# Gated attention unit with a cosine-gated two-layer product on one core: consecutive tokens per partition, v rows padded apart, and three moved scores

## Chip, cores and metric

The kernel runs on one core of one Trainium2 chip (trn2). The metric is the device time of an execution in microseconds; lower is better. Verdicts are "faster", "same" or "slower" at 2%.

## The reference

```python
def _attn_ref(u, v, z):                       # u, v: 8 x 3008 x 256, z: 8 x 3008 x 64
    scale = 1.0 / S
    scores = scale * np.matmul(z, z.transpose(0, 2, 1))
    attn = np.maximum(scores, 0.0) ** 2
    out = np.matmul(attn, v)
    return (u * out).astype(np.float32)

def _moe_ref(x, w_in, w_out):                 # x: 24064 x 256, w_in: 256 x 2048, w_out: 2048 x 256
    h = x @ w_in
    g = h * np.cos(h)
    return (g @ w_out).astype(np.float32)
# reference = _moe_ref(_attn_ref(u, v, z).reshape(24064, 256), w_in, w_out)
```

Inputs and output are float32. The scores are symmetric, and the sum over tokens in the attention doesn't depend on the order of the tokens, as long as z, v, u and the output rows all use the same order. The first part of the change uses that.

## The kernel before

Each batch of 3008 tokens is cut into 24 blocks of 128 (the last has 64) and six columns of four blocks. A column J of a batch is a slot; there are 48. For one column, PE makes scores (two 64-row matmuls side by side, "a score" below), ScalarE takes relu (`r`), VectorE squares (`A`), and PE multiplies the pieces of `A` with v in "value pairs" (two 64-row matmuls each). Half of the `A` pieces are had by a DMA transposition of the other half, as the scores are symmetric. Then the gate with u gives x, `emit_h` makes h = x·w_in, ScalarE and VectorE make g = h·cos(h), and y = g·w_out follows. The first three columns of batch 0 run by `phase_a_first`, for which nothing is prepared yet. In the lines of the profile `E` and `M` are tiles in PSUM, the memory that matmuls write (a piece of it that one matmul fills is a bank here), `zT` is the transposed z, and `sm` the sum of attention results that the gate uses (the gate sum).

Token order in the loads (u and v, and the last rows apart):

```python
def load_rows(t, src, b, g):
    full = 4 if g < NC - 1 else 3
    nc.gpsimd.dma_start(
        t[:, 0:full, :],
        src[b, g * CW:g * CW + full * P, :].rearrange("(j p) d -> p j d", p=P),
    )
    # ... the last 64 tokens are put in both halves of the partitions

def load_v(b, g):
    t = vpool.tile([P, 4, D], FP16, name="v16")
    load_rows(t, v, b, g)
    vs[b, g] = t
```

The first three columns, with the places of the scores:

```python
def phase_a_first(s, n, extra={}):
    # ... takes banks; steps = value pairs (dh, k), 46 of them, then the last block
    lo, hi = 5 if s == 0 else 2, 42
    at = {}
    for i in range(n):
        p = lo + (hi - lo) * i // (n - 1)
        at[p] = at.get(p, 0) + 1
    for i, (dh, k) in enumerate(steps):
        # ... the value pair
        if dh > 0 and (k % 4 == 3):
            drop_piece((b, J, k // 4))
            if s > 0:
                emit_turns((0, 0), 1)          # one DMA transposition of A
                if k < 4:
                    turn_u(s)
                # ...
        for _ in range(at.get(i, 0)):
            emit_score(later=squares if s == 0 and i == lo else None)
    # ...
    late_sums.extend(gate_sum(s, *acc[dh]) for dh in range(2))
    hold(late_sums[0][0:1, 0:1])               # a GpSimd copy that waits for the gate sum
    load_u(s + 1)
```

The calls of the three columns and what stands between them (the queue of w_out's load is GpSimd's, in order, so the load comes behind the `hold` and the u load at the end of the second column, s = 1):

```python
phase_a_first(0, 12, {4: lambda: turn_late(4), 8: lambda: turn_late(5)})
phase_a_first(1, 12)
nc.gpsimd.dma_start(w_out16, moe_w_out.rearrange("(k p) f -> p k f", p=P))
for i in range(2):
    emit_h(0, i)()
phase_a_first(2, 14)
# ...
phase_b(2)                                     # h of slots 0 and 1, and the first y: the first use of w_out
```

Of the kernel before, what the change touches and what calls it, by code (L numbers as in the profile page):

```python
# [9 lines left out]
FP16 = mybir.dt.float16  # L10
# [4 lines left out]
def kernel(  # L15
# [9 lines left out]
    nc = tc.nc  # L25
# [3 lines left out]
    B, S, D = u.shape  # L29
    dqk = z.shape[2]  # L30
    Dff = moe_w_in.shape[1]
    P = 128
    H = P // 2
    CW = 512
    NB = (S + P - 1) // P
    NC = (S + CW - 1) // CW
    WL = S - (NC - 1) * CW
    NFT = Dff // P
    NSLOT = B * NC
    NPC = 18  # L40
    assert D == 2 * P and dqk == H and S - (NB - 1) * P == H and NB == 4 * NC
    assert B % 2 == 0 and WL == 3 * P + H and NFT == 16

    inv_s2 = (1.0 / float(S)) * (1.0 / float(S))
    half_pi = float(math.pi / 2.0)
# [8 lines left out]
    vpool = pool("v", 7)  # L54
# [39 lines left out]
    def drop_piece(key):  # L94
        i = pieces.pop(key)
        if pending.get(i):
            pending[i] = "dropped"
        else:
            free_pieces.append(i)
# [8 lines left out]
    halves = [(0, NB // 2), (NB // 2, NB)]  # L108
    z16s, zTs, vs, u16s, uTs, xs, gs = {}, {}, {}, {}, {}, {}, {}
    yps = {}  # L110

    def load_z(b, half):
        lo, hi = halves[half]
        z16 = zpool.tile([P, NB // 2, P], FP16, name="z16")
        z16s[b] = z16
        full = min(hi, NB - 1)
        for h in range(2):
            nc.gpsimd.dma_start(
                z16[:, 0:full - lo, h * dqk:(h + 1) * dqk],
                z[b, lo * P:full * P, :].rearrange("(j p) d -> p j d", p=P),  # L120
            )
            if hi == NB:
                for r in range(2):
                    nc.gpsimd.dma_start(
                        z16[r * H:(r + 1) * H, hi - lo - 1, h * dqk:(h + 1) * dqk],
                        z[b, (NB - 1) * P:S, :],
                    )
# [10 lines left out]
    def load_rows(t, src, b, g):  # L138
        full = 4 if g < NC - 1 else 3
        nc.gpsimd.dma_start(  # L140
            t[:, 0:full, :],
            src[b, g * CW:g * CW + full * P, :].rearrange("(j p) d -> p j d", p=P),
        )
        if full == 3:
            for r in range(2):
                nc.gpsimd.dma_start(t[r * H:(r + 1) * H, 3, :], src[b, S - H:S, :])

    def load_v(b, g):
        t = vpool.tile([P, 4, D], FP16, name="v16")
        load_rows(t, v, b, g)  # L150
        vs[b, g] = t

# [104 lines left out]
    def emit_value(b, J, k, t, dh, bank, start, stop):  # L257
        nc.tensor.matmul(  # L258
            bank[:, 0:width(J)],
            vs[b, k // 4][t * H:(t + 1) * H, k % 4, dh * P:(dh + 1) * P],  # L260
            value_rhs(b, J, k, t),
            start=start,
            stop=stop,
        )
# [82 lines left out]
    def phase_a_first(s, n, extra={}):  # L347
        b, J = s // NC, s % NC
        ea = e_order.pop(0)
        pair = [E[ea][:, 0, :], E[ea][:, 1, :]]  # L350
        acc = [pair, M] if s == 1 else [M, pair]
        last = NB - 1
        run = 1 if s == 0 else 2
        steps = [
            (dh, k)
            for I in range(0, NC, run)
            for dh in range(2)
            for k in range(4 * I, min(4 * (I + run), last))
        ] + [(2, last)]
        lo, hi = 5 if s == 0 else 2, 42  # L360
        at = {}
        for i in range(n):
            p = lo + (hi - lo) * i // (n - 1)
            at[p] = at.get(p, 0) + 1
        for i, (dh, k) in enumerate(steps):
            if i in extra:
                extra[i]()
            if dh == 2:
                emit_value(b, J, last, 0, 0, acc[0][0], False, True)
                emit_value(b, J, last, 1, 1, acc[1][1], False, True)  # L370
            else:
                for t in range(2):
                    emit_value(
                        b, J, k, t, dh, acc[dh][t], k == 0, k == last - 1 and t != dh
# [4 lines that stand above are left out]
                    emit_turns((0, 0), 1)  # L379
                    if k < 4:  # L380
                        turn_u(s)
                    elif k < 8:
                        for d in range(2):
                            gate_mul(s - 1, d, late_sums.pop(0))
            for _ in range(at.get(i, 0)):
                emit_score(later=squares if s == 0 and i == lo else None)
        if s == 0:
            turn_u(0)
        late_sums.extend(gate_sum(s, *acc[dh]) for dh in range(2))
        hold(late_sums[0][0:1, 0:1])  # L390
        load_u(s + 1)
        e_order.append(ea)
# [30 lines left out]
    T = 2 * P  # L423
# [109 lines left out]
    def emit_y(m, i):  # L533
        for ft in range(2 * i, 2 * i + 2):
            for k in range(mwidth(m) // P):
                y_block(m, ft, k)

    def store_half(m, half, o):
        b, J = m // NC, m % NC
        n = min(2, mwidth(m) // P - 2 * half)  # L540
        t0 = b * S + J * CW + half * T
        if J == NC - 1 and half == 1 and n == 2:
            nc.sync.dma_start(out[t0:t0 + P, :], o[:, 0, :])
            nc.sync.dma_start(out[t0 + P:t0 + P + H, :], o[0:H, 1, :])
            nc.sync.dma_start(out[b * S - H:b * S, :], o[H:P, 1, :])
        else:
            nc.sync.dma_start(
                out[t0:t0 + n * P, :].rearrange("(k p) d -> p k d", p=P), o[:, 0:n, :]
            )

    def store_y(m):
        for half in range(2):
# [9 lines left out]
    def last_y(m):  # L562
        b, J = m // NC, m % NC
        for ft in range(NFT):
            y_block(m, ft, 0)
            y_block(m, ft, 1)
        for k in range(4):
            if k >= 2:
                for ft in range(NFT):
                    y_block(m, ft, k)  # L570
            o = opool.tile([P, 2, D], FP32, name="o")
            nc.scalar.activation(
                o[:, 0, :], y_bank(m, k),
                AF.Copy, bias=0.0, scale=inv_s2,
            )
            t0 = b * S + J * CW + k * P
            if k < 3:
                nc.sync.dma_start(out[t0:t0 + P, :], o[:, 0, :])
            else:
                nc.sync.dma_start(out[t0:t0 + H, :], o[0:H, 0, :])  # L580
                nc.scalar.dma_start(out[b * S - H:b * S, :], o[H:P, 0, :])

    def phase_b(s):
# [46 lines left out]
    for g in range(NC):  # L630
        eng = nc.sync if g % 2 == 0 else nc.scalar
        full = 4 if g < NC - 1 else 3
        eng.dma_start(
            z32[g][:, 0:full, :],
            z[0, g * CW:g * CW + full * P, :].rearrange("(j p) d -> p j d", p=P),
        )
        if full == 3:
            for r in range(2):
                nc.sync.dma_start(z32[g][r * H:(r + 1) * H, 3, :], z[0, S - H:S, :])
# [87 lines left out]
    for s in range(3, NSLOT + 1):  # L727
        b, J = s // NC, s % NC
# [52 lines left out]
```

## Time and profile before

| what | value |
|---|---|
| time, median of the first three runs | 1193.71 us (1193.34 to 1194.58) |
| span of the profiled run | 1191.4 us |
| matmuls on PE | 11887, busy 99% of the span |
| VectorE, ScalarE, GpSimd busy | 85%, 67%, 58% |
| DMA packets | 479862 |

The page lists the DMA queues as packets, megabytes and the time that their packets took, as a share of 16 engines' span:

```profile
DMA packets 479862, 148.00 MB, mean 124 GB/s; under 512 B 404208, under 2 KB 479472, under 8 KB 479728
...
q1 hardware_dynamic: 380752, 112.93, 54.4%
q0 software_dynamic: 97440, 32.78, 27.3%
```

q1 carries the transpositions and the stores, q0 the loads from GpSimd. Together they keep the 16 engines 82% busy, beside a PE that is 99% busy. Whole views are read in the prediction below.

### The profile page before, as it was taken

Reading aid. Unit: us, or ns where it says so; the run is one execution under the profiler, and the core shown is the slowest. Engines: PE = TensorE matmul, PEld = TensorE weight load, DVE = VectorE, ACT = ScalarE, POOL = GpSimd, SP = SyncE. Lnnn points to the kernel's source line nnn. Section 1 sums busy time; section 2 is a strip of 40 time slices with the busy share of each in tenths; the row PEclk is TensorE's granted clock in tenths of the full one; section 3 lists DMA queues with packets and bytes.
Section 4 is the critical chain, followed back from the end, with each engine's and each line's share of the span. In section 5 each row is a group of like instructions: output and inputs, shape, how many; then the busy total and the mean of one; then the engine's idle time right before and its main releaser. Section 6 shows DMA issues by size and latency. Waiting matters only on the chain.

```text
span 1191.4 us, 29044 instructions
## 1 busy us (share of the span) xinstructions
PE 1183.3 (99%) x11887; PEld 727.2 (61%) x11887; DVE 1012.3 (85%) x1302; ACT 794.9 (67%) x927; POOL 690.5 (58%) x717
## 2 busy tenths in 40 slices
PE   9999999999999999999999999999999999999998
PEld 4556665665566656666566665656666566665566
DVE  6899888889988898888988889888888888888776
ACT  7966676667666676667676676666766666666454
POOL 3287746657466573755647556476565665545452
PEclk9999999999999999999999999999999999999999
DMA  9999998569995699946999459973898737964301
GB/s 160 172 170 163 138 147 131 102 121 134 143 130 98 123 140 162 131 84 104 157 147 135 85 104 161 169 119 72 122 164 149 122 71 123 166 125 86 65 20 54
DMA packets 479862, 148.00 MB, mean 124 GB/s; under 512 B 404208, under 2 KB 479472, under 8 KB 479728
## 3 DMA queue, kind: packets, MB, share of 16 engines
q1 hardware_dynamic: 380752, 112.93, 54.4%
q0 software_dynamic: 97440, 32.78, 27.3%
q8 instruction: 93, 1.52, 0.5%
q10 hardware_dynamic: 1536, 0.43, 0.2%
q14 instruction: 41, 0.34, 0.1%
HBM read 66.32 MB, written 24.64 MB: 76 GB/s over the span
## 4 chain that ended last, share of the span: by engine, by line
PE 97%; ACT 1%; DVE 1%; issue 0%; POOL 0%; DVEq 0%; ACTq 0%
PE E L404 27%; PE M L482 23%; PE M L258 20%; PE E L258 19%; PE E L194 5%; PE M L525 1%; ACT r L204 1%; PE M L460 1%; DVE g L415 0%; PE E L664 0%; DVE sm L270 0%; PE E L525 0%; POOL s L433 0%; ACT c L412 0%; DVE o L495 0%
## 5 line engine op out<-in xcount | busy, mean ns | idle before, releaser
L412 ACT ACTIVATE c<-E 128x1024 f16<-128x1024 f32 (+1 forms) x384 | 385.7, 1007 | 216.4 <-PE E L404 214.1
L415 DVE SCALAR_TENSOR_TENSOR g<-E,c 128x1024 f16<-128x1024 f32 (+1 forms) x384 | 458.4, 1195 | 60.6 <-ACT c L412 59.5
L204 ACT ACTIVATE r<-E 128x512 f16<-128x512 f32 (+1 forms) x342 | 327.9, 967 | 112.7 <-PE E L194 106.5
L258 PEld LDWEIGHTS <-v 64*128 64x128 f16 x4512 | 246.3, 94 | 229.3 <-issue 19.4
L404 PE MATMUL E<-x,w_in 128*128 128x512 f16 (+1 forms) x1408 | 354.0, 375 | 0.0
L433 POOL TENSOR_TENSOR s<-g 128x512 f16<-128x512 f16 (+1 forms) x184 | 208.3, 1132 | 188.5 <-DVE g L415 138.7
L258 PE MATMUL M<-A,v 64*128 64x512 f16 (+1 forms) x2256 | 283.0, 372 | 0.2 <-DVE o L495 0.2
L258 PE MATMUL E<-A,v 64*128 64x512 f16 (+1 forms) x2256 | 278.1, 371 | 0.0
L434 POOL TENSOR_TENSOR g<-g 128x512 f16<-128x512 f16 (+1 forms) x184 | 219.5, 1193 | 14.4
L404 PEld LDWEIGHTS <-w_in 128*128 128x128 f16 x1536 | 133.1, 98 | 108.9 <-issue 19.5
L482 PEld LDWEIGHTS <-g 128*128 128x128 f16 x2816 | 172.5, 98 | 40.8
L209 DVE TENSOR_TENSOR A<-r 128x1024 f16<-128x1024 f16 x240 | 174.0, 737 | 15.0 <-ACT r L204 14.3
L286 POOL TENSOR_TENSOR x<-sm,uT 128x512 f16<-128x512 f32 (+1 forms) x43 | 48.6, 1132 | 212.9 <-DVE sm L270 212.5
L482 PEld LDWEIGHTS <-s 128*128 128x128 f16 x2112 | 129.4, 98 | 32.1 <-DVE s L440 0.5
L194 PE MATMUL E<-zT 64*128 64x512 f16 (+4 forms) x684 | 127.6, 355 | 2.0 <-DVE sm L270 0.7
L440 DVE TENSOR_TENSOR s<-s,g 128x1024 f16<-128x1024 f16 (+1 forms) x92 | 100.6, 1094 | 2.1 <-POOL s L433 2.1
L482 PE MATMUL M<-w_mix,s 128*128 128x128 f16 x1408 | 94.0, 219 | 0.3 <-POOL s L433 0.3
L482 PE MATMUL M<-w_mix,g 128*128 128x128 f16 x1408 | 93.6, 219 | 0.0
L482 PE MATMUL M<-w_out,g 128*128 128x128 f16 x1408 | 93.6, 219 | 0.0
L212 DVE TENSOR_TENSOR A<-r 128x512 f16<-128x512 f16 (+1 forms) x102 | 79.6, 781 | 8.9 <-ACT r L204 8.1
L194 PEld LDWEIGHTS <-zT 64*128 64x128 f16 x684 | 38.8, 94 | 38.5 <-issue 4.0
L442 DVE TENSOR_TENSOR s<-g,s 128x1024 f16<-128x1024 f16 (+1 forms) x92 | 60.5, 660 | 0.0
(58 smaller groups left out, 646.9 us busy)
## 6 DMA issues: line engine op xcount, KB each, us to landing
out_dram<-o SPq DMA_DIRECT2D x87, 256.0 KB, 2.2
v<-in_v_dram POOLq DMA_DIRECT2D x40, 256.0 KB, 8.8
u<-in_u_dram POOLq DMA_DIRECT2D x40, 256.0 KB, 4.8
A<-A SPq DMA_TRANSPOSE x252, 5.1
z<-in_z_dram POOLq DMA_DIRECT2D x14, 192.0 KB, 10.6
z<-in_z_dram POOLq DMA_DIRECT2D x14, 176.0 KB, 5.9
v<-in_v_dram POOLq DMA_DIRECT2D x8, 192.0 KB, 11.9
u<-in_u_dram POOLq DMA_DIRECT2D x8, 192.0 KB, 4.1
```

The costliest lines, as they stand in the source:

```text
L194: nc.tensor.matmul(e[:, t, 0:Wt], zT[rows, k * P:(k + 1) * P], zT[rows, J * CW:J * CW + Wt], start=True, stop=True,)
L204: nc.scalar.activation(r[:, :, 0:W], e[:, :, 0:W], AF.Relu)
L209: nc.vector.tensor_tensor(a4, r4, r4, ALU.mult)
L212: nc.vector.tensor_tensor(a4, r[:, :, 0:W], r[:, :, 0:W], ALU.mult)
L258: nc.tensor.matmul(bank[:, 0:width(J)], vs[b, k // 4][t * H:(t + 1) * H, k % 4, dh * P:(dh + 1) * P], value_rhs(b, J, k, t), start=start, ...
L404: nc.tensor.matmul(e[:, f, 0:W], w_in16[:, k, ft * P:(ft + 1) * P], x[:, k, 0:W], start=(k == 0), stop=(k == 1),)
L412: nc.scalar.activation(c[:, :, 0:W], e[:, :, 0:W], AF.Sin, bias=half_pi, scale=inv_s2)
L415: return lambda: nc.vector.scalar_tensor_tensor(gs[m][:, 2 * i:2 * i + 2, 0:W], e[:, :, 0:W], 1.0, c[:, :, 0:W], ALU.mult, ALU.mult)
L433: nc.gpsimd.tensor_tensor(s1[:, f, 0:n], g[:, f, low], g[:, lower, low], ALU.add)
L434: nc.gpsimd.tensor_tensor(g[:, f, low], g[:, f, up], g[:, f, low], ALU.subtract)
L440: nc.vector.tensor_tensor(s2[:, f, 0:n], s1[:, f, 0:n], g[:, f, up], ALU.subtract)
L482: nc.tensor.matmul(acc[:, k * P:(k + 1) * P], left[:, ft, k * P:(k + 1) * P], right[:, ft, :], start=(ft == 0 and k == 0), stop=(ft == F - ...
```

## The change

The intent is fewer and larger DMA packets, and shorter stalls of PE in the second and third column. Three parts:

1. A partition holds 12 (first half of a batch) or 11 consecutive tokens instead of every 128th. The rows that a partition gets of u, of the first z and of the output then lie together in DRAM.
2. v's tile gets 16 unused columns per row, so that the v rows of a partition don't join into one packet on the chip's side.
3. Scores stand three value pairs further back: the second column's second one (behind pair 8 instead of 5), and the third column's first two (behind 5 and 8 instead of 2 and 5); the third column's third goes from behind pair 8 to behind 9.

```diff
+    def half_rows(rows, half):
+        lo, hi = halves[half]
+        n = min(hi, NB - 1) - lo
+        return rows[lo * P:(lo + n) * P, :].rearrange("(p j) d -> p j d", p=P)
+
+    def group_rows(rows, g):
+        first = 4 * (g % 3)
+        return half_rows(rows, g // 3)[:, first:first + (4 if g < NC - 1 else 3), :]
...
             t[:, 0:full, :],
-            src[b, g * CW:g * CW + full * P, :].rearrange("(j p) d -> p j d", p=P),
+            group_rows(src[b], g),
...
     def load_v(b, g):
-        t = vpool.tile([P, 4, D], FP16, name="v16")
+        t = vpool.tile([P, 4, D + 16], FP16, name="v16")[:, :, 0:D]
...
             p = lo + (hi - lo) * i // (n - 1)
+            if s > 0 and i < 2:
+                p = (2, 8)[i] if s == 1 else (5, 9)[i]
             at[p] = at.get(p, 0) + 1
...
-                out[t0:t0 + n * P, :].rearrange("(k p) d -> p k d", p=P), o[:, 0:n, :]
-            )
+            nc.sync.dma_start(rows[:, 2 * half:2 * half + n, :], o[:, 0:n, :])
...
-            z[0, g * CW:g * CW + full * P, :].rearrange("(j p) d -> p j d", p=P),
+            group_rows(z[0], g),
```

(The loads of later z, the last rows and the last stores are rewritten in the same way. Line numbers move: value matmuls L258 become L266, scores L194 become L202, h matmuls L404 become L414, first y matmuls L525 become L535, w_out's load L712 becomes L723.)

More of the change, by code (lines that the diff above doesn't have):

```diff
@@ L41 @@
     assert D == 2 * P and dqk == H and S - (NB - 1) * P == H and NB == 4 * NC
-    assert B % 2 == 0 and WL == 3 * P + H and NFT == 16
+    assert NC == 6 and B % 2 == 0 and WL == 3 * P + H and NFT == 16
     inv_s2 = (1.0 / float(S)) * (1.0 / float(S))
@@ L115, in load_z @@
         z16s[b] = z16
-        full = min(hi, NB - 1)
+        n = min(hi, NB - 1) - lo
         for h in range(2):
             nc.gpsimd.dma_start(
-                z16[:, 0:full - lo, h * dqk:(h + 1) * dqk],
-                z[b, lo * P:full * P, :].rearrange("(j p) d -> p j d", p=P),
+                z16[:, 0:n, h * dqk:(h + 1) * dqk], half_rows(z[b], half)
             )
@@ L536, in emit_y, with out_rows @@
                 y_block(m, ft, k)
+    def out_rows(m):
+        b, J = m // NC, m % NC
+        return group_rows(out[b * S:(b + 1) * S, :], J)
     def store_half(m, half, o):
-        b, J = m // NC, m % NC
+        b = m // NC
+        rows = out_rows(m)
         n = min(2, mwidth(m) // P - 2 * half)
-        t0 = b * S + J * CW + half * T
-        if J == NC - 1 and half == 1 and n == 2:
-            nc.sync.dma_start(out[t0:t0 + P, :], o[:, 0, :])
-            nc.sync.dma_start(out[t0 + P:t0 + P + H, :], o[0:H, 1, :])
+        if m % NC == NC - 1 and half == 1 and n == 2:
+            nc.sync.dma_start(rows[:, 2, :], o[:, 0, :])
+            nc.sync.dma_start(out[(b + 1) * S - H:(b + 1) * S, :], o[0:H, 1, :])
             nc.sync.dma_start(out[b * S - H:b * S, :], o[H:P, 1, :])
         else:
-            nc.sync.dma_start(
-                out[t0:t0 + n * P, :].rearrange("(k p) d -> p k d", p=P), o[:, 0:n, :]
-            )
+            nc.sync.dma_start(rows[:, 2 * half:2 * half + n, :], o[:, 0:n, :])
     def store_y(m):
@@ L575, in last_y @@
             )
-            t0 = b * S + J * CW + k * P
             if k < 3:
-                nc.sync.dma_start(out[t0:t0 + P, :], o[:, 0, :])
+                nc.sync.dma_start(out_rows(m)[:, k, :], o[:, 0, :])
             else:
-                nc.sync.dma_start(out[t0:t0 + H, :], o[0:H, 0, :])
+                nc.sync.dma_start(out[(b + 1) * S - H:(b + 1) * S, :], o[0:H, 0, :])
                 nc.scalar.dma_start(out[b * S - H:b * S, :], o[H:P, 0, :])
```

## The prediction

> **What bounds the kernel now.** I read the page first, then the waits of the matrix engine, then the timeline of its first 54 us with the starts of each matmul, and the DMA packets last.
>
> ```profile
> PE 1183.3 (99%) x11887; PEld 727.2 (61%) x11887; DVE 1012.3 (85%) x1302; ACT 794.9 (67%) x927; POOL 690.5 (58%) x717
> DMA  9999998569995699946999459973898737964301
> PE 97%; ACT 1%; DVE 1%; issue 0%; POOL 0%; DVEq 0%; ACTq 0%
> ```
>
> The matrix engine is busy 99% of 1191.4 us and makes 97% of the chain of waits; the DMA row is almost as full. Which of the two sets the end is told by the waits of PE, all that there are:
>
> ```profile
> PE E L664 <- DVE s L627: 1.2, 1, 1.2
> PE E L194 <- DVE sm L270: 0.7, 1, 0.7
> PE E L194 <- DVE g L415: 0.4, 1, 0.4
> PE E L194 <- ACT zT L657: 0.4, 1, 0.4
> PE M L482 <- POOL s L433: 0.3, 1, 0.3
> PE E L194 <- DVE zT L659: 0.2, 1, 0.2
> PE M L258 <- DVE o L495: 0.2, 1, 0.2
> PE E L194 <- ACT r L204: 0.2, 1, 0.2
> ```
>
> No line names a DMA: PE never waits for a transfer directly, in spite of the full DMA row. The only waits that a DMA ends near PE are at the start, in the waits of VectorE: `DVE z L645 <- DMA z<-in_z_dram` is 3.0 us in 2 times. So transfers can matter before the first transposition, and nowhere else as things stand.
>
> The busy row hides waits, since a matmul's end is modelled, so I took starts. A 512-column matmul over 128 rows starts 216 ns after the one before, and two 64-row ones share such a step (108 ns each). Summed over the kernel, the starts exceed this beat by only 17.7 us: 3.3 before 8.6 us, 0.8 from there to 23, 1.1 to 38.1, 1.7 to 53, then 0.9 per 100 us without exception. The last is the change between 64-row and 128-row work (47 of L258 to L404 at 0.2 us extra, 46 back at 0.1), which this edit does not touch. So what can be won at all is a part of about 7 us at the start.
>
> **What the Trainium skill says.** "TensorE: Matmul & The Clock Gate", section "Wait — 56ns, not 53.3ns?", gives warm start-to-start as N ÷ 2.4 GHz plus about 2.5 ns, 215.7 ns at 512 columns; the trace agrees (216). "Perfetto Trace Analysis", in its opening note, calls matmul busy time a bad metric since matmuls are pipelined; the trace agrees: the wait at 24.1 us below is 0.84 us by starts and 0.66 us by the idle column. "DMA: Bandwidth & Descriptors", section "Why small descriptors are slow (HBM only)", names a fixed overhead per packet; the trace agrees: a 256-byte packet took 20 ns at the start and a 1024-byte store 49 ns, 12.5 ns per 256 bytes.
>
> **The change part by part.** No arithmetic changes, and each engine has as many instructions as before.
>
> Part one, tokens. A partition gets 12 (or 11) consecutive tokens instead of every 128th. The first z loads then carry 4 rows of 256 bytes as one 1024-byte run, the u loads 4 rows of 1024 as one run, the stores of two output rows 2048 bytes. v rows stay single, as the new padding stops them from joining; the later z loads stay single because their rows are written to alternate 128-byte places. Packets: u 40×512 + 8×384 = 23552 become 48×128 = 6144; stores 87×256 = 22272 become 11136; first z 5×512 + 384 = 2944 become 768. That is 30720 fewer of 479862, so 449142. Estimated from the durations above, the DMA share of 82% loses some 4 points. Since PE never waits for it after the start, I count all that as zero.
>
> At the start it can count:
>
> ```profile
> 0.73 1.56 SPq L633 DMA_DIRECT2D z<-in_z_dram  x3
> 1.19 3.17 PE L664 MATMUL E<-s 128*128 128x512 f16 x7 [1.19 <-DVE s L627]
> 3.91 0.80 DVE L645 CAST z<-z 128x512 f16<-128x512 f32 x2 [2.78 <-DMA z<-in_z_dram]
> 4.39 0.77 PE L649 MATMUL turned<-id,z 128*128 128x128 f16 x8
> 4.93 0.59 ACT L657 COPY zT<-turned 128x512 f16<-128x512 f16 x1 [0.89 <-PE turned L649]
> 6.01 3.77 ACT L204 ACTIVATE r<-E 128x1024 f16<-128x1024 f32 x4 [0.49 <-PE E L194]
> ```
>
> The first z group lands at 3.89, its cast starts 0.02 later, and PE transposes at 4.39. With a quarter of the packets I estimate landing about 0.5 us sooner. But PE is not free then: the last of seven warm-up matmuls starts at 3.72 and they step by 427 ns, so nothing starts before 4.15. The gain is 4.39 − 4.15 = 0.24 us, whatever more the DMA saves. The chain behind it (copy, score, four activations) moves with it. v's first group lands at 8.12, before its use at 8.64, and should land earlier still, with less z traffic ahead of it.
>
> Part two, second column (s = 1). Its second score moves from behind value pair 5 to behind pair 8 (counted from 0).
>
> ```profile
> 23.26 0.40 PE L194 MATMUL E<-zT 64*128 64x512 f16 x2
> 23.47 0.83 PE L258 MATMUL E<-A,v 64*128 64x512 f16 x6
> 24.96 0.39 PE L194 MATMUL E<-zT 64*128 64x512 f16 x2 [0.66 <-DVE sm L270]
> 26.04 0.40 PE L194 MATMUL E<-zT 64*128 64x512 f16 x2
> ```
>
> The second score needs the bank that the gate sum of the column before reads until 24.91. Three pairs after 23.47 end at 24.12, so PE stands 0.84 us. With three pairs more it comes at 24.77 and waits 0.19. The third score, one pair behind, then starts at 24.96 + 0.22 + 0.22 = 25.39 instead of 26.04. That is 0.65 us ahead, but ScalarE must empty two banks in turn: its activation of the second score still starts at 25.39 and takes 1.03, so the fourth score, due at 26.25, waits for 26.47 (0.22). Left: 0.65 − 0.22 = 0.43 us. From there ScalarE can follow: in a backlog its activations start every 0.905 us, and this column asks for one per 1.0.
>
> Part three, third column (s = 2). First score from behind pair 2 to behind pair 5, second from 5 to 8, third from 8 to 9.
>
> ```profile
> 38.13 1.21 PE L258 MATMUL M<-A,v 64*128 64x512 f16 x6
> 39.77 0.39 PE L194 MATMUL E<-zT 64*128 64x512 f16 x2 [0.43 <-DVE g L415]
> 40.90 0.39 PE L194 MATMUL E<-zT 64*128 64x512 f16 x2
> 41.76 0.40 PE L194 MATMUL E<-zT 64*128 64x512 f16 x2
> ```
>
> Now PE stands 0.69 before the first and 0.27 before the second, both for the two products g of 1.2 us on VectorE. Moved, the first is due at 39.73 and starts at 39.77, the second still has to wait for 40.90, the third can start at 41.33 rather than 41.76. So 0.43 us looks won. I think that most is given back. Activations here start at 42.26, 43.18, 44.08, 44.98, 45.89, 46.79: no gap, 0.905 us apart, while the scores come every 0.86. Before, the ninth and tenth scores (46.99, 47.91) start 0.05 us after the seventh and eighth activations end (46.94, 47.86): by then ScalarE paces PE. The activations of scores one and two do not move by this edit, so the eighth ends at most 0.04 us earlier and the tenth score with it. Gain: 0.04 us, the rest swallowed by waits on ScalarE between scores four and ten.
>
> Sum: 0.24 + 0.43 + 0.04 = 0.71 us; 1193.71 − 0.71 = 1193.0 us.
>
> **Rivals.** (a) All of the placement gains stay: 0.24 + 0.65 + 0.63 = 1.5 us, 1192.2. For it: a score behind pair 9 finds PE far ahead, and small slips of ScalarE may have slack that I don't see. Against: the gapless activations. (b) ScalarE takes back the second column's gain too, or the start's landing does not improve: some 0.3 us, 1193.4. Against: gaps of 0.05 us before every third activation of that column. (c) Larger packets hold up the DMA transpositions of A that share the engines, and PE gets a wait for A: some 1 to 3 us more. For it: the DMA row of 9s and 5.1 us median per transposition. Against: fewer packets and less engine time in all, and no DMA wait now. (d) DMA relief shows in the body: several us. Against: the constant 0.9 us per 100 us; there is no DMA wait to take away. Also, the pitch of v (544 bytes instead of 512) could change its weight loads (94 ns); they lie beside matmuls.
>
> **Range and chances.** Three runs of before spread over 1.2 us, as much as the effect. From (a) with luck to (b) with a small part of (c): 1191.9 to 1194.2. Two per cent is 24 us, over three times all that the start holds. Faster by over 2%: 0.005; within: 0.985; slower (a strong form of (c)): 0.01.
>
> **What would show it.** Page: about 449 thousand packets, DMA row lower, PE still 99%. Start: first transposition at about 4.15; if it stays at 4.39 or the cast still starts at 3.9, the first step is wrong. Second column: a wait of about 0.2 us before the second score and a new one on an activation before the fourth; column 0.4 us shorter from 23.26. Third column: the DVE wait gone, waits on ACT in its place, the length from 38.1 to the first L404 behind it about unchanged; shortened by 0.4 or more, rival (a) holds. Any PE wait named after a DMA or after A speaks for (c), a fall of the 0.9 us per 100 us for (d); either would make the prediction wrong.

## The result, and the profile after

| kernel | runs, us | median |
|---|---|---|
| before, six runs | 1194.58, 1193.34, 1193.71, 1194.80, 1193.99, 1195.15 | 1194.28 |
| changed, six runs | 1196.83, 1199.05, 1193.20, 1193.58, 1196.91, 1192.81 | 1195.20 |

The ratio is 1.0009, 95% interval 0.9989 to 1.003: the same. A ratio here and below is the mean time of one kernel's runs over the mean of the other's in the same rounds, so it isn't quite the ratio of the medians. The median of 1195.20 lies outside the predicted range of 1191.9 to 1194.2. The runs fall in two groups: three at 1192.8 to 1193.6, which is where the prediction put them, and three at 1196.8 to 1199.1, all less than 1.5% above the fastest. The profiled execution (1196.83) is one of the longer ones, so its trace shows what the longer ones have.

The page of the changed kernel (busy row; packets and queues as above; the chain that ended last, by engine):

```profile
PE 1185.7 (99%) x11887; PEld 727.1 (61%) x11887; DVE 1012.7 (85%) x1302; ACT 794.5 (66%) x927; POOL 679.8 (57%) x717
...
DMA packets 449142, 148.00 MB, mean 124 GB/s; under 512 B 401264, under 2 KB 432496, under 8 KB 449008
...
q1 hardware_dynamic: 368464, 112.93, 56.9%
q0 software_dynamic: 80032, 32.78, 27.1%
...
PE 95%; DMA 2%; issue 1%; ACT 1%; DVE 0%; POOL 0%; ACTq 0%; POOLq 0%
```

The packet count is the predicted one exactly. The DMA share didn't fall by some 4 points; it rose from 81.7% to 84.0%. And in the chain a DMA stands with 2% of the span where before there was none. The waits of PE name it (total us, times, longest):

```profile
PE M L535 <- DMA w_out<-in_moe_w_out_dram: 2.4, 1, 2.4
...
PE E L202 <- ACT r L212: 0.4, 2, 0.2
```

One wait, once: the first y matmul for the w_out weights. The former waits for `sm` (0.7) and `g` (0.4) before scores are gone. Here is the same place in both kernels, PE's timeline (start, us, line, tiles, form, count, idle before). Before:

```profile
52.77 1.90 PE L404 MATMUL E<-x,w_in 128*128 128x512 f16 x8
54.51 1.04 PE L525 MATMUL M<-w_out,g 128*128 128x256 f16 x8
55.38 1.03 PE L404 MATMUL E<-x,w_in 128*128 128x512 f16 x4
```

After:

```profile
52.34 1.90 PE L414 MATMUL E<-x,w_in 128*128 128x512 f16 x8
56.66 1.88 PE L535 MATMUL M<-w_out,g 128*128 128x256 f16 x8 [2.41 <-DMA w_out<-in_moe_w_out_dram]
58.33 1.91 PE L414 MATMUL E<-x,w_in 128*128 128x512 f16 x4
```

Two things are to be seen. The changed kernel comes to this place 0.43 us sooner (52.34 against 52.77); eight matmuls of 216 ns on, at 54.07, PE is ready for y, and stands until 56.66, 2.6 us. And after the stand the same matmuls take almost twice as long: the first eight y matmuls 1.88 us against 1.04, the next four h matmuls 1.91 against 1.03. A table by stretches shows why (us, then busy time and count of PE, PEld, DVE, ACT and POOL, then the granted clock, DMA share and GB/s; packets in flight at the same time are added up, so the share can be over 1). After:

```profile
54.10:56.60 2.50, 0.15 (x1) 0.00 (x0) 2.50 (x3) 1.32 (x2) 0.62 (x2) 1.00 1.32 188
56.70:60.10 3.40, 3.40 (x13) 1.76 (x14) 0.19 (x1) 0.00 (x0) 0.00 (x0) 0.50 1.23 251
```

Before:

```profile
56.70:60.10 3.40, 3.40 (x24) 2.14 (x22) 2.71 (x3) 2.69 (x3) 3.40 (x4) 1.00 0.95 125
```

The granted clock was 0.50 in the stretch behind the stand, and 13 matmuls are counted in it where before there were 24. By the clock records it was low from 56.70 to 60.11. So a wait of 2.6 us cost about 4.2: at matmul 290, counted from 0, (38.34 against 38.75) the changed kernel is 0.41 ahead, at 460 (64.74 against 60.91) it is 3.8 behind, and 3.6 at the last (1190.33 against 1186.74). That single place makes the difference of the two profiled runs; what lies before and behind it is in the changed kernel's favour.

Why was w_out late? GpSimd's timeline where it is issued, before:

```profile
39.20 1.16 POOL L712 DMA_DIRECT2D w_out<-in_moe_w_out_dram  x1
```

After:

```profile
38.57 1.18 POOL L723 DMA_DIRECT2D w_out<-in_moe_w_out_dram  x1
```

And its time from issue to landing, in the DMA view of this stretch (KB each, us), before and after:

```profile
w_out<-in_moe_w_out_dram POOLq DMA_DIRECT2D x1, 1024.0 KB, 14.9
```

```profile
w_out<-in_moe_w_out_dram POOLq DMA_DIRECT2D x1, 1024.0 KB, 18.0
```

Before, w_out landed at 39.20 + 14.92 = 54.12, and its first use came at 54.51. The margin was 0.39 us, and that is why no list of waits named it: a wait list shows only what was late, not what was nearly late. After, it was issued 0.63 us sooner, took 3.1 us longer, landed at 56.61, and the use was due at 54.07. 

The packet records of the traces tell what holds it up. w_out is 2048 packets of 512 bytes. Where it has the engines alone, 320 to 390 of them pass per microsecond (before, 46 to 48 us); beside a transposition of `A` it is about 240 of each, one for one (before at 51.5 to 53 us, after at 53.5 to 54.5, and in w_ahead_of_u below from 43 to 48). The Trainium skill, "DMA: Bandwidth & Descriptors", section "Queues, rings and completion order", says that an engine takes its queues in turn, a packet at a time; the equal counts agree with that. On top there is a stretch at 49 to 52.5 us in which few packets pass and most half-microseconds have means of 110 to 770 ns instead of 20 to 70, in both queues, beside one 16-KB packet that fetches instructions and itself took 3.5 us; before, such a stretch lasted 1.5 us and the fetch took 0.97 us. In a run where w_out is due with 0.4 us to spare, its length decides.

What else was predicted can be read in the same trace. Second column after:

```profile
24.99 0.39 PE L202 MATMUL E<-zT 64*128 64x512 f16 x2
...
25.42 0.39 PE L202 MATMUL E<-zT 64*128 64x512 f16 x2
...
26.50 0.39 PE L202 MATMUL E<-zT 64*128 64x512 f16 x2
```

Second, third and fourth score start at 24.99, 25.42 and 26.50; predicted were 24.96, 25.39 and 26.47. Third column:

```profile
39.36 0.44 PE L202 MATMUL E<-zT 64*128 64x512 f16 x2
...
40.49 0.39 PE L202 MATMUL E<-zT 64*128 64x512 f16 x2
...
40.92 0.39 PE L202 MATMUL E<-zT 64*128 64x512 f16 x2
...
41.99 0.39 PE L202 MATMUL E<-zT 64*128 64x512 f16 x2 [0.25 <-ACT r L212]
```

The stalls for `g` are gone, and already the fourth score waits for ScalarE. From matmul 290 to the first h matmul behind it, the third column took 14.02 us before (38.75 to 52.77) and 14.00 after (38.34 to 52.34).

### The profile page after: what moved, and what is told of

It is laid out like the page before. It is cut to its first block, busy times and chain, and to the rows that moved or that the text cites. A ratio compares the mean times of both kernels' runs of the same rounds, so it can differ in the third digit from the quotient of the medians.

```text
span 1195.0 us, 29044 instructions
## 1 busy us (share of the span) xinstructions
PE 1185.7 (99%) x11887; PEld 727.1 (61%) x11887; DVE 1012.7 (85%) x1302; ACT 794.5 (66%) x927; POOL 679.8 (57%) x717
## 4 chain that ended last, share of the span: by engine, by line
PE 95%; DMA 2%; issue 1%; ACT 1%; DVE 0%; POOL 0%; ACTq 0%; POOLq 0%
PE E L414 27%; PE M L492 23%; PE M L266 19%; PE E L266 18%; PE E L202 5%; DMA w_out<-in_moe_w_out_dram 2%; PE M L535 1%; ACT r L212 1%; PE M L470 1%; PE E L675 0%; PE E L535 0%; DVE g L425 0%; POOL s L443 0%; POOL u L148 0%; ACT c L422 0%
## 5 line engine op out<-in xcount | busy, mean ns | idle before, releaser
L266 PEld LDWEIGHTS <-v 64*128 64x128 f16 x4512 | 245.7, 94 | 229.1 <-issue 18.8
L414 PE MATMUL E<-x,w_in 128*128 128x512 f16 (+1 forms) x1408 | 354.9, 375 | 0.0
L266 PE MATMUL M<-A,v 64*128 64x512 f16 (+1 forms) x2256 | 283.0, 372 | 0.0
L266 PE MATMUL E<-A,v 64*128 64x512 f16 (+1 forms) x2256 | 278.1, 371 | 0.0
L414 PEld LDWEIGHTS <-w_in 128*128 128x128 f16 x1536 | 133.3, 98 | 109.4 <-issue 20.1
L202 PE MATMUL E<-zT 64*128 64x512 f16 (+4 forms) x684 | 127.6, 355 | 1.0 <-ACT r L212 0.4
L202 PEld LDWEIGHTS <-zT 64*128 64x128 f16 x684 | 39.0, 94 | 38.7 <-issue 4.1
```

What stands on the lines that cost most here:

```text
L202: nc.tensor.matmul(e[:, t, 0:Wt], zT[rows, k * P:(k + 1) * P], zT[rows, J * CW:J * CW + Wt], start=True, stop=True,)
L266: nc.tensor.matmul(bank[:, 0:width(J)], vs[b, k // 4][t * H:(t + 1) * H, k % 4, dh * P:(dh + 1) * P], value_rhs(b, J, k, t), start=start, ...
L414: nc.tensor.matmul(e[:, f, 0:W], w_in16[:, k, ft * P:(ft + 1) * P], x[:, k, 0:W], start=(k == 0), stop=(k == 1),)
```

## The experiments

The theory after the result (D in the texts): the parts do what was predicted, some 0.7 us together, but w_out lands within tenths of its first use in both kernels, and in those runs in which it comes late PE stands, may lose its clock, and loses up to 4 us and more. Its rivals: that the layout itself slows the transfers or the body (L), that the placement of the scores makes w_out late (P), and chance between runs (N). In the texts of turns_held and w_ahead_of_u three more letters stand for what makes w_out late: S, that its packets and a transposition's take turns; F, the slow stretch around the fetch of instructions; U, the joined u packets ahead of it in the queue. Each kernel was run beside the kernel before on the same chip. All gave correct results. All edits are against the changed kernel, unless it says otherwise.

### after_w_early: w_out's load one column sooner

```diff
-    phase_a_first(1, 12)
     nc.gpsimd.dma_start(w_out16, moe_w_out.rearrange("(k p) f -> p k f", p=P))
+    phase_a_first(1, 12)
```

> Changed kernel with only the load of w_out issued one column earlier, at about 25 us instead of 38.6. Theory D (the slow runs are those in which w_out lands after its first use at 54 us): w_out lands by about 45 us, no PE wait names a DMA, all runs lie within 1.5 us of each other near 1193.0, none near 1197. Rival L (the new token order slows transfers or the engines somewhere else, in some runs): still two groups of runs, near 1193 and near 1197. Rival P (the placement of the scores shifts the transpositions ahead of w_out and so on): also cured here, to be told apart by the two half changes.

Measured: 1192.68, 1192.65, 1192.24, 1192.78, 1192.63; median 1192.65 against 1193.42 of before (nine runs), ratio 0.9994 (0.9981 to 1.0006). The two groups have become one, within 0.54 us. The trace, first GpSimd's timeline, then PE's:

```profile
25.06 1.18 POOL L722 DMA_DIRECT2D w_out<-in_moe_w_out_dram  x1
```

```profile
52.21 1.90 PE L414 MATMUL E<-x,w_in 128*128 128x512 f16 x8
53.94 1.04 PE L535 MATMUL M<-w_out,g 128*128 128x256 f16 x8
54.82 1.03 PE L414 MATMUL E<-x,w_in 128*128 128x512 f16 x4
```

w_out landed at 36.42, 17 us ahead of its use. The y matmuls follow without a stand at full clock. This is what D says, and L, which expected two groups of runs still, can't give it. P would be cured here too, as its text says; the two half changes below tell it apart.

### before_w_early: the same move in the kernel before

```diff
-    phase_a_first(1, 12)
     nc.gpsimd.dma_start(w_out16, moe_w_out.rearrange("(k p) f -> p k f", p=P))
+    phase_a_first(1, 12)
```

(against the kernel before)

> Kernel before with only the load of w_out issued one column earlier. Theory D: its runs narrow too and lie at 1193.3 to 1193.8 (its fastest runs now), since its margin was 0.4 us (landing 54.12, use 54.51) and some of its runs must have missed it; the changed kernel with the same edit is 0.4 to 0.6 us faster than this one, which is what the moved scores are worth. Rival (the kernel before never misses the landing): its spread of 1193.3 to 1195.2 stays as it is.

Measured: 1193.10, 1193.09, 1192.89, 1193.32, 1193.09; median 1193.09, ratio 0.9998 (0.9985 to 1.0012). The move alone gains about nothing where w_out was on time anyway, and its runs lie within 0.43 us, against 1.13 of the nine runs of before beside them, none of which was long. With the race out of both kernels, the change is worth 1193.09 − 1192.65 = 0.44 us by the medians, and by the start of the last matmul 1186.64 − 1185.92 = 0.72 us. Predicted were 0.71, but the parts aren't the predicted ones, so the agreement of the sum is luck: of the 0.72, 0.08 lie before matmul 150, 0.44 in the second column, 0.01 in the third and 0.18 around 96 us, where a wait of the kernel before is gone; predicted were 0.24, 0.43, 0.04 and nothing. And it is the difference of two single traces: in w_early_again, the same kernel once more, the last matmul starts at 1186.15, which makes it 0.49, as its start was slower (see "The start" below). The intervals of the ratios are wider than that (0.0012 of 1193 is 1.4 us), so the timed runs alone don't prove a gain; the steps in the traces below show where it lies.

### layout_only and scores_only: each part alone, w_out where it was

layout_only:

```diff
-            if s > 0 and i < 2:
-                p = (2, 8)[i] if s == 1 else (5, 9)[i]
```

> Changed kernel with the old score places. Theory D: PE reaches the first use of w_out at about 54.5, as before, so slow runs are rarer than in the full change but can occur; fast runs near 1193.6 (0.45 more than the full change's 1193.0). Rival L: slow runs near 1197 in half of the runs. Rival P: no slow runs, spread as before.

scores_only, against the kernel before:

```diff
+            if s > 0 and i < 2:
+                p = (2, 8)[i] if s == 1 else (5, 9)[i]
```

> Kernel before with the new score places alone. Theory D: PE reaches the first use at 54.07, so runs near 1193.2 where w_out is there and 1194 to 1199 where it is not; as many slow ones as in the full change. Rival L: no slow runs, all near 1193.2. Rival P: slow runs as in the full change. Waits in the second and third column as in the changed kernel.

Measured: layout_only 1197.43, 1192.64, 1192.65, 1192.87, 1192.78, ratio 1.0003 (0.9989 to 1.0017); scores_only 1193.50, 1194.11, 1197.03, 1193.75, 1196.79, ratio 1.0014 (1.0002 to 1.0027). Both have runs of either group. The profiled run of layout_only, PE's timeline:

```profile
53.80 1.24 PE L412 MATMUL E<-x,w_in 128*128 128x512 f16 x5
57.17 1.05 PE L533 MATMUL M<-w_out,g 128*128 128x256 f16 x8 [2.13 <-DMA w_out<-in_moe_w_out_dram]
58.06 1.65 PE L412 MATMUL E<-x,w_in 128*128 128x512 f16 x4
59.50 1.92 PE L533 MATMUL M<-w_out,g 128*128 128x256 f16 x8
```

That of scores_only:

```profile
54.76 1.05 PE L527 MATMUL M<-w_out,g 128*128 128x256 f16 x8 [0.58 <-DMA w_out<-in_moe_w_out_dram]
```

In layout_only PE was ready at 53.80 + 5 × 0.216 = 54.88 and stood 2.3 us; the clock fell from 58.32 to 61.73 (the second group of y matmuls takes 1.92 us). In scores_only it stood 0.7 us and the clock stayed. So neither part alone is needed for a late w_out, nor does either prevent it; L and P, each as the only cause, are out.

### after_again: the changed kernel once more, on another chip

> The changed kernel once more, to see its two groups of runs on the same chip as the next three and to get a second profile. If the lateness of w_out is a matter of chance in each execution: about one run in two or three near 1196 to 1199, the rest 1192.3 to 1193.5. If it belonged to the first chip: one group.

Measured: 1192.85, 1197.45, 1193.03, 1193.79, 1194.12, 1195.54; median 1193.96 against 1193.26 of eleven runs of before, ratio 1.0004 (0.9989 to 1.0018). Its profiled run has a short wait:

```profile
54.45 1.05 PE L535 MATMUL M<-w_out,g 128*128 128x256 f16 x8 [0.33 <-DMA w_out<-in_moe_w_out_dram]
```

Among those eleven runs of the unchanged kernel, on the same chip, were 1197.34 and 1195.36. So long runs aren't the change's own. Counted over all, 1195 us or more came in 5 of 12 runs of the changed kernel, in 3 of 35 of the kernel before, in 3 of 10 of the two partial ones, and in none of the 30 runs of the six series (five kernels) that have w_out's load one column sooner (a seventh, with v joined, is slow for another reason and not counted).

### w_ahead_of_u: w_out just ahead of the u load

```diff
+        if s == 1:
+            nc.gpsimd.dma_start(w_out16, moe_w_out.rearrange("(k p) f -> p k f", p=P))
         load_u(s + 1)
...
-    nc.gpsimd.dma_start(w_out16, moe_w_out.rearrange("(k p) f -> p k f", p=P))
```

> Changed kernel, w_out issued just ahead of the third u load instead of just behind it: 0.5 us earlier at issue, and the 2-KB packets of u are behind it. Rival U (the joined u packets hold w_out up): w_out lands 1 to 2 us earlier, near 53 to 54, few or no slow runs. Theory S: the order of these two changes little, since the transpositions still take turns with it: still slow runs, perhaps fewer.

Measured: 1192.95, 1193.82, 1193.35, 1194.24, 1194.40, 1194.02; median 1193.92, ratio 1.0 (0.9988 to 1.0012). No run is in the upper group, and w_out landed at 51.29, 2.6 us before its use. From its issue to its first packet it took 2.0 us here (37.63 to 39.67), where behind the u load it took 4.9 in after and 5.1 in before. By the expectation's own test this speaks for the u load in front (U) and against S, which expected long runs still; with one trace and six runs, against 7 of 12 of the changed kernel that weren't long either, it isn't proof. That the u packets are joined can't be what is needed, as scores_only, with single u rows, had a late w_out too. But only two of the six runs are in the lower group. PE's timeline:

```profile
53.94 0.38 PE L537 MATMUL M<-w_out,g 128*128 128x256 f16 x2
54.78 0.81 PE L537 MATMUL M<-w_out,g 128*128 128x256 f16 x6 [0.46 <-DVE sm L278]
```

and, from the waits of all engines:

```profile
DVE A L217 <- DMA A<-A: 1.5, 1, 1.5
```

Now a transposition of `A`, which shares the engines with w_out, landed late (52.74); VectorE waited for it, its gate sum came later, and PE stood about 0.6 us for a bank that the gate sum still read. One wait was turned into another. Both lie in the same crowded stretch of 15 us.

### turns_held: the transpositions kept out of w_out's way

```diff
-                    emit_turns((0, 0), 1)
+                    if s == 1 and k < 12:
+                        emit_turns((0, 0), 1)
```

> Changed kernel, in which the fourth and fifth transposition of A of the second column and those of the third are issued only after the third column, so that w_out has the DMA engines to itself from about 44 us. Theory S (packets of w_out and of a transposition take turns one for one, and this is what makes it late): w_out lands before 51 us in every run, no PE wait for it, all runs within 1.5 us at 1192.5 to 1193.2, unless the held transpositions make a wait of their own later, which would be named after A or an activation. Rival F (a slow stretch of all packets around the fetch of instructions at 49 us makes it late by itself): still slow runs.

Measured: 1200.16, 1200.92, 1202.52, 1200.82, 1203.58, 1201.02; median 1200.97, ratio 1.0063 (1.005 to 1.0076). The transpositions were to run after the third column. w_out did land sooner for it, at 53.65, and no wait for it is left. It didn't come as soon as it could: only its last 36 packets started after 50.0, but they fell into a slow stretch there. The edit brought waits of its own, a transposition that came late and behind it a bank:

```profile
DVE A L220 <- DMA A<-A: 7.3, 2, 7.0
...
PE E L415 <- DVE sm L278: 5.3, 1, 5.3
```

The clock was at half from 89.06, within this stand of 5.3 us, to 95.89. This costs more than it saves, and its time says nothing of w_out; only the landing does. As a test it is inconclusive.

### layout_w_early: the layout alone, with w_out early

```diff
-            if s > 0 and i < 2:
-                p = (2, 8)[i] if s == 1 else (5, 9)[i]
...
-    phase_a_first(1, 12)
     nc.gpsimd.dma_start(w_out16, moe_w_out.rearrange("(k p) f -> p k f", p=P))
+    phase_a_first(1, 12)
```

> New token order and padding, old score places, w_out issued one column earlier. No wait on w_out. Against the whole change with w_out early (1192.65) it misses the placement, by the traces 0.45 us: 1193.0 to 1193.1; the gain over the kernel before with w_out early (1193.09) is then only that of the start, 0.1 us. If it comes to 1192.7 instead, as the fast runs of the layout alone did, the layout has a gain of 0.3 us that I have not found.

Measured: 1192.55, 1193.00, 1193.31, 1193.27, 1193.44; median 1193.27, ratio 0.9993 (0.9981 to 1.0004). No long run, and no sign of the hidden gain of 0.3 us that 1192.7 would have meant.

### w_early_again and second_col_w_early: what each column's places are worth

w_early_again is the kernel of after_w_early once more:

```diff
-    phase_a_first(1, 12)
     nc.gpsimd.dma_start(w_out16, moe_w_out.rearrange("(k p) f -> p k f", p=P))
+    phase_a_first(1, 12)
```

> The changed kernel with w_out issued one column earlier, once more, as the measure for the next three on the same chip: one group of runs, 1192.2 to 1193.5, none near 1196.

second_col_w_early keeps only the second column's places:

```diff
-            if s > 0 and i < 2:
-                p = (2, 8)[i] if s == 1 else (5, 9)[i]
+            if s == 1 and i < 2:
+                p = (2, 8)[i]
...
-    phase_a_first(1, 12)
     nc.gpsimd.dma_start(w_out16, moe_w_out.rearrange("(k p) f -> p k f", p=P))
+    phase_a_first(1, 12)
```

> As w_early_again with the third column's scores at their old places and the second column's at the new ones. My step (ScalarE takes the third column's gain back): the stretch from the start of the third column to the first matmul on w_out is longer by 0.0 to 0.1 us only. Rival (a) of the prediction (the gain stays): longer by 0.4 to 0.6 us.

Measured: 1192.65, 1192.35, 1192.54, 1192.42, 1193.27 (median 1192.54, ratio 0.9994) and 1192.62, 1192.40, 1192.55, 1192.39, 1192.80 (median 1192.55, ratio 0.9993): no difference. The starts of matmuls measure the columns much more finely than the times of runs (PE's records of the traces, us, matmuls counted from 0; the stretch from matmul 150 to 290 holds the second column's moved scores, that from 290 to 420 those of the third):

| kernel | 150 | 290 | 420 | second column | third column |
|---|---|---|---|---|---|
| before_w_early | 21.31 | 38.72 | 54.81 | 17.42 | 16.08 |
| layout_w_early | 21.00 | 38.41 | 54.50 | 17.42 | 16.08 |
| second_col_w_early | 21.39 | 38.37 | 54.45 | 16.98 | 16.08 |
| w_early_again | 21.45 | 38.42 | 54.49 | 16.98 | 16.07 |
| after_w_early | 21.22 | 38.20 | 54.27 | 16.98 | 16.07 |

The second column's places are worth 0.44 us, within 0.01 of what was predicted, and the layout nothing there. The third column's are worth 0.01; ScalarE takes the rest back. Matmul 150, which carries the start, varies by 0.45 us in this table; "The start" below shows with what.

### v_joined_w_early: v without the padding

```diff
-        t = vpool.tile([P, 4, D + 16], FP16, name="v16")[:, :, 0:D]
+        t = vpool.tile([P, 4, D], FP16, name="v16")
...
-    phase_a_first(1, 12)
     nc.gpsimd.dma_start(w_out16, moe_w_out.rearrange("(k p) f -> p k f", p=P))
+    phase_a_first(1, 12)
```

> As w_early_again without the padding of v, so that v rows join to 2-KB packets too. If the padding matters for the weight loads: the mean of 94 ns for them changes. If it matters for the landing of the first v group (7.9 to 8.1 us, use at 8.6): a landing after 8.6 and a PE wait on v. If neither: same time within 0.3 us, since no PE wait names v.

Measured: 1217.16, 1208.36, 1212.22, 1211.55, 1214.49; median 1212.22, ratio 1.0162 (1.0141 to 1.0184): far outside the noise. That was not expected: the padding is worth 19.7 us of this layout (1212.22 − 1192.54). From the trace, v's landing and then the wait of PE, joined:

```profile
v<-in_v_dram POOLq DMA_DIRECT2D x40, 256.0 KB, 18.9
```

```profile
PE M L266 <- DMA v<-in_v_dram: 15.6, 16, 2.6
```

and the landing in w_early_again, with the padding:

```profile
v<-in_v_dram POOLq DMA_DIRECT2D x40, 256.0 KB, 11.3
```

With joined rows a v load comes as packets of 2048 bytes and lands after 18.9 us instead of 11.3, and PE waits for v 16 times. A single v load joined landed sooner (5.1 against 7.3 us at 102 us); it is the five loads of a batch in a row, beside transpositions, that land late. There (128 to 150 us) a 2048-byte packet took 305 ns on average, no less than four of 512 bytes in w_early_again (4 × 79), and the transpositions' packets 94 ns instead of 48. Why the mixture lands so late isn't isolated by any run here. The waits for v and two stretches at half clock (296.90 to 300.31 and 600.68 to 604.10) account for most of the 24.5 us that separate the two profiled runs. The other two things that the padding might have mattered for did not: v's weight loads took 93.8 ns against 93.5, and the first v group landed at 8.13, before its use at 8.84.

### warm6_w_early: one warm-up matmul fewer

```diff
-    for i in range(7):
+    for i in range(6):
...
-    phase_a_first(1, 12)
     nc.gpsimd.dma_start(w_out16, moe_w_out.rearrange("(k p) f -> p k f", p=P))
+    phase_a_first(1, 12)
```

The prediction said that PE isn't free for the first transposition before 4.15, as the warm-up matmuls step by 0.43 us. If so, z landing early is worth more with one fewer.

> As w_early_again with six warm-up matmuls instead of seven. My step (the warm-up holds the first transposition to 4.15 when z lands early): the first transposition starts between 3.75 and 4.15 where z lands by 3.4, and the first score 0.1 to 0.4 us sooner, the end likewise. Rival (the landing of z, or the cast and copy behind it, holds the start): the first score starts at 5.4 to 5.5 as before, no gain.

Measured: 1192.17, 1192.42, 1192.65, 1192.18, 1192.41; median 1192.41 against 1193.35 of before, ratio 0.9992 (0.9979 to 1.0004), the lowest median of all, though not by more than the spread. The start of its trace:

```profile
4.01 1.03 PE L660 MATMUL turned<-id,z 128*128 128x128 f16 x8
```

The same in after_again, with seven:

```profile
4.15 0.88 PE L660 MATMUL turned<-id,z 128*128 128x128 f16 x8
```

The transposition starts 0.14 us and the first score, at 5.29 instead of 5.46, 0.17 us sooner. In after_again z had landed by 3.28 and PE was busy until 4.15, as predicted; with six it is the cast of z, begun at 3.52, that sets the start.

## Why the prediction was right and wrong

**The step that failed** is the sentence "Since PE never waits for it after the start, I count all that as zero", and before it the reading of the waits, "No line names a DMA: PE never waits for a transfer directly". Both are true of the trace of before and were taken for more than they say. That list shows transfers that were late. w_out was 0.39 us from being one of them (landed at 54.12, used from 54.51), and it could have been found by setting landings against first uses. The sum made each part's effect on PE right, and left out that PE's being 0.43 us sooner, and other traffic in the same stretch, act on a transfer without slack. The term that was set to zero measured 4.2 us in the profiled run, 2.6 of standing and the rest from the clock, and 0.5 and 0.7 us of standing, by starts, in the milder ones (after_again and scores_only).

**Rival (c)** had the right sort of cause, "PE gets a wait for A: some 1 to 3 us more", and the wrong transfer: PE waited for w_out, not for `A`, and it lost more than 3 us as no one had counted the clock. Its reason was larger packets that hold up transpositions. A packet of 256 bytes on the transpositions' queue took 28.2, 28.0 and 27.8 ns on average in after, after_again and w_early_again against 26.2 and 26.6 in before and before_w_early, so something of that is real, without a wait of PE for `A`. The prediction's own test was that any PE wait named after a DMA would make it wrong; that is what the waits showed.

**The DMA share** was to fall by some 4 points and rose by 2.3 (the traces with the layout have 83.3 to 85.6, those without it 81.6 to 82.3). By the packet records: u's rows and v's and w_out's of 512 bytes took 18.9 points before; now the 512-byte ones take 10.4 and u's joined ones 7.8, a relief of 0.7 only, as a 2048-byte packet took 251 ns where four of 512 bytes take 288. The stores gave 0.65 (6.2 to 5.6). The z packets of 128 bytes, in unchanged number, took 0.5 more, and the transpositions' packets 3.2 more. The step that was wrong is the scaling from few durations at the start and of the stores to packets in the crowd. It moved no matmul by itself, as far as the runs show.

**What was right.** The packet count of 449142. The second column: 0.43 predicted, 0.44 measured, with the starts of three scores within 0.03 us. The third: 0.04 predicted, 0.01 measured, so rival (a) is out. The body: between matmul 800 (98.76 in before, 102.34 in after) and the last (1186.74, 1190.33) the lag stays at 3.58 to 3.59 us, so not a hundredth is gained or lost there, and rival (d), a gain throughout the body, is out. Only between 600 and 800 do 0.25 us go, most of it the one wait `DVE o L495` of 0.2 us at 96 us, which is gone with the layout and wasn't predicted. Of rival (b), ScalarE didn't take back the second column's gain, but the start did give less than was counted on.

**The start** was to gain 0.24 us and gained about half of it. The first part of the step is right: z landed 0.3 to 0.6 us sooner in all traces with the layout but one, and in eight of the ten with the layout and seven warm-up matmuls the transposition starts at 4.15, as predicted. But the next sentence, that the chain behind it moves with it, doesn't hold: the first score starts at 5.46 in these eight, 0.12 before the 5.58 of before (before_w_early has 5.54, scores_only 5.53). The lines of after_again, to be set against those of before in the prediction, where the copy follows 0.54 us behind the transposition (4.93 behind 4.39) and the score starts at 5.58:

```profile
4.82 0.58 ACT L668 COPY zT<-turned 128x512 f16<-128x512 f16 x1 [1.06 <-PE turned L660]
5.46 0.61 PE L202 MATMUL E<-zT 64*128 64x512 f16 x4 [0.43 <-ACT zT L668]
```

Here the copy follows 0.67 behind. The clock records say why. In before the first record of full clock begins at 4.66, in after_again at 4.71; until then the transposing matmuls step by 107 ns, from then on by 56. Starting sooner, more of them run at half clock. The moment differs from run to run, and most of what the start varies by goes with it, here in the ten traces with the layout and seven warm-up matmuls (us):

| trace | full clock from | matmul 150 |
|---|---|---|
| layout_w_early | 3.98 | 21.00 |
| after_again | 4.71 | 21.23 |
| after_w_early | 4.82 | 21.22 |
| w_ahead_of_u | 5.45 | 21.22 |
| after | 5.50 | 21.36 |
| second_col_w_early | 5.83 | 21.39 |
| w_early_again | 5.97 | 21.45 |
| v_joined_w_early | 6.76 | 21.54 |
| layout_only | 7.12 | 21.71 |
| turns_held | 7.14 | 21.72 |

Where before has full clock from about the same moment as after_again, 4.66 and 4.71, the layout is worth 0.11 us (21.34 against 21.23). In the profiled run of the result z landed late as well, at 3.81, and the first score started at 5.60; in layout_w_early, with full clock from 3.98, the transposition started at 4.07 and the score at 5.13. So the prediction took 0.24 for the gain of the start where these traces have 0.1, beside a variation of 0.7 us that it didn't know of.

**What stays open.** Whether the change makes a late w_out more likely, or whether the first six runs had bad luck. In those six 3 were long, against 1 of 6 of before; in after_again 2 of 6 against 2 of 11, and its median, 1193.96, lies inside the predicted range. So the side of the range on which a median of six falls hangs on how many runs come late. All together, 5 of 12 against 3 of 35, leans towards the change, but the first six are among them, which raised the question. A reason can be argued: w_out's packets now start at 43 instead of 44 us and so share the engines for longer with a transposition, which landed at 50.5, 49.1 and 49.4 in three traces with the moved scores and at 48.7 before (but at 49.2 in layout_only, without them); and PE needs w_out 0.43 us sooner. w_ahead_of_u says that the u load in front of w_out has a part in it, in both kernels. No run isolates the rest. Nor is it shown what makes the slow stretch in the packets. Half-microseconds in which the transpositions' packets average over 100 ns lie within 1.5 us of an instruction fetch in 55 of 64 cases in before, 71 of 86 in after and 57 of 60 in before_w_early, while 34 to 35% of all half-microseconds with such packets do; that is a coincidence in time, not a proof. And that all the long runs are long for w_out is inferred from their absence in 30 runs with the early load; traces were only taken of two of them, and both show it.

## What to carry to other kernels

A wait list shows what was late, not what was nearly late: for each transfer that is loaded once, set its landing against its first use, and where the margin is a fraction of a microsecond, issue it sooner, which here cost one moved line and left no long run in 30. When a kernel's times fall in two groups, look for such a race before you explain the median. And before moving work to fill a stall of PE, look at the engine that must take the result: where ScalarE's activations already followed each other without a gap, 0.43 us of apparent gain became 0.01. At the start of a kernel, ask at which clock PE runs before you carry a gain along a chain: here 0.24 us became about 0.1.

## What the Trainium skill lacked or had wrong

- "TensorE: Matmul & The Clock Gate", section "Why this matters for your kernels", advises against PE-idle gaps of more than about 3 us. Here gaps of 2.6 us (after) and 2.3 us (layout_only) were already followed by 3.41 us at a granted clock of 0.50 (56.70 to 60.11, and 58.32 to 61.73), which cost some 1.6 us on top of the first; gaps of 0.7 us (scores_only) and 0.5 us (after_again, by starts) were not. In v_joined_w_early a gap of 2.6 us (at 296.8 us) was followed by it and one of 2.2 us (at 898.8) was not.
- "Perfetto Trace Analysis", section "What “DMA-bound” means", says that large descriptors are what matters where DMA engines bind. In this kernel, joining v's rows into 2048-byte packets moved the median landing of v from 11.3 to 18.9 us and the time from 1192.54 to 1212.22 us, and joining u's made four rows only 13% cheaper (251 ns against 4 × 72 ns). What it lacks is the case of large packets beside many small ones of transpositions, in a kernel that PE bounds.
- No page has it that packets of both busy queues can be slow together for 1.5 to 3.5 us: means of 110 to 770 ns in most half-microseconds instead of 20 to 70, in the neighbourhood of a 16-KB instruction fetch that took 0.97 us in one trace and 3.5 us in another. The cause isn't shown here.
